# Two 128-byte pads in SBUF and a new order of the router's dot products in the last dense pass

## Chip, core and metric

The kernel runs on one core of a Trainium2 chip. The metric is device time in microseconds for one execution. Before the change the median of three runs is 737.13 us (736.93 to 737.21).

## What is computed

The reference chains three parts over 1,536 tokens of width 512. Only the last two bear on the change:

```python
x = attention(q, k, v, lam)                      # decayed linear attention, N=1536 x D=512
p = domain_probs / domain_probs.sum(-1)          # dense mixture, 4 experts
x = sum(p[:, e] * (relu(x @ w1[e]) @ w2[e]) for e in range(4))
logits = x @ w_gate                              # router of the second mixture, 8 experts
expert = argmax(logits); gate = softmax(logits)[expert]
out[token] = gate * (relu(x[token] @ v1[expert]) @ v2[expert])
```

The dense mixture sends every token through four experts with 1,024 hidden columns. The second mixture sends a token to one of eight experts, so the router's choice for every token must be known before its rows can be gathered by expert.

## The kernel before, in words

Tokens are held in 12 tiles of 128: tiles 0 to 5 are the first half, 6 to 11 the second. The accumulator `acc` (L100) holds per tile 512 sums and two more columns, the gate and the token's number. Matmuls are in fp32r, each product split in a high and a low part, so a product takes three matmuls.

The dense mixture runs in passes over half experts. The first pass and the last are plain; the 13 passes between them are "fast units" (`fast_unit`, matmuls on L754) with fewer products, on sums of operands: their moving operands are the halves of `xh`, `xl` and the tiles `t1` to `t4` of 384 columns. The **last pass** handles the second half of the tokens in three pairs of tiles. Each pair runs eight hidden products `h` (`moe1_mm1`, 12 matmuls of 256 columns each, L600), and then two output products (`moe1_mm2`: `y`, 24 matmuls of 512 columns, L600; for the last three tiles `last_dense`: `yz`). Below the tiles of the three pairs are a and b (6 and 7), c and d (8 and 9), y and z (10 and 11).

PSUM is given out from a ring of three banks (`ps_mm`): a product needs the bank of the third product before it, and that bank is free only when VectorE (DVE) has read it last. Behind a hidden product ScalarE (ACT) makes the high part (L607) and VectorE the low part `ht_..l` (L608); behind an output product VectorE adds it to `acc` (L641; L672 for `last_dense`).

After each product a **hook** runs steps that are written out by hand in a table, `plan`. In the last pass hook 0 to 7 stand behind the hidden products of the first pair, 8 and 9 behind its outputs; 10 to 19 are the second pair's; 20 to 27 are the hidden products of the third. Hooks `(KL - 2, 18)` and `(KL - 2, 19)` stand behind the last two outputs of the last fast unit. What a hook issues goes into each engine's queue in that order, and each engine works its queue strictly in order.

The steps of the table:

- `logit_v` (L866), called a **router sum** here: one VectorE instruction that multiplies a tile's 512 columns of `acc` with one expert's router row and adds them up, with a short read of the total behind it. A tile needs eight of them, one for each expert. For tiles a, b and c they follow the tile's last addition to `acc`. For d, y and z they are made on `acc` as it is before the last pass's addition, and the matmuls of `last_dense` supply the rest; they must only come before that addition. Router rows 0 to 2 lie in tiles `row0` to `row2` (loaded by `open_last`, L840), the others in `x2`. The load inside `logit_v` runs for tile 5 alone.
- `route_choose` (L928 to L946): maximum, choice and one-hot of a tile, six short VectorE instructions and one on GpSimd (POOL).
- `route_send` (L950 to L983): two tiny matmuls for the rank (L953, L955), one ScalarE exponential, three short VectorE instructions, four short GpSimd instructions, and a GpSimd scatter of the tile's rows (L123). The routed half starts with a load of what all scatters of tiles 0 to 9 have written.
- `wg_columns`: the router's columns for `last_dense`.

Of the kernel before, what the change touches and what calls it, by code (L numbers as in the profile page):

```python
# [8 lines left out]
F32 = mybir.dt.float32  # L9
# [9 lines left out]
P = 128  # L19
# [23 lines left out]
KL = K1 - 1  # L43
# [33 lines left out]
def body(ctx: ExitStack, tc: tile.TileContext, lam, att, dp, w1a, w2a, wgt, w1b, w2b, out):  # L77
# [3 lines left out]
    def pool(name, bufs, **kw):  # L81
        return tc.tile_pool(name=name, bufs=bufs, **kw)
# [5 lines left out]
    accp = ctx.enter_context(pool("accp", 1))  # L88
# [9 lines left out]
    ones = const.tile([P, P], BF16, name="ones")  # L98
    desc = const.tile([P, E2], F32, name="desc")
    acc = accp.tile([P, NC, W], F32, name="acc")  # L100
    rk_all = const.tile([P, NC], F32, name="rk_all")
    m2_all = const.tile([P, NC], F32, name="m2_all")
    tiles_e = const.tile([P, E2], F32, name="tiles_e")
# [698 lines left out]
    def open_routing():  # L802
        op = ctx.enter_context(pool("order", 1, side="right"))
        for name, n, d in (
            ("places", EN, F32), ("caps", EN, F32), ("count", E2, F32), ("place", EN, F32),
            ("cap_e", E2, F32), ("lw", 2 * FC * E2, F32), ("nth", EN, I32),
            ("tmp", E2 * max(OMAX, E2), F32),
        ):
            od[name] = op.tile([P, n], d, name=name)
        G.iota(  # L810
            od["places"], pattern=[[1, EN]], base=0, channel_multiplier=0,
            allow_small_or_imprecise_dtypes=True,
        )
        G.memset(od["cap_e"][:, 0:1], float(CAPS[0]))
        for i in range(EN):
            G.memset(od["caps"][:, i:i + 1], float(BY_RANK[i]))
        rp = rt["rs"] = ctx.enter_context(pool("rs", 2, side="right"))
        rt["sm"] = [rt_ctx.enter_context(pool("ps_sm", 1, space=PSUM))]
        rt["none"] = rp.tile([P, W - DM], F32, name="none", bufs=1)
        G.memset(rt["none"], 0.0)  # L820
        G.memset(rt["none"].bitcast(I32)[:, 1:], FAR)
# [308 lines left out]
    with tc.manual_schedule():  # L1130
# [104 lines left out]
        def att_rest():  # L1235
            c = done.pop("rest", None)
            if c is not None:
                att_within(c, 1)
                at_t.pop((c, "v"))
                load_kv(c + 3, "v")  # L1240
                done["c"] = c
            if done["c"] == NC - 1 and "end" not in done:
                done["end"] = 1
                at_ctx.close()
                open_routing()
                open_fast()
# [49 lines left out]
        def at(hook, what, *args):  # L1296
            plan.setdefault(hook, []).append(lambda: what(*args))
# [11 lines left out]
        a, b, c = TT, TT + 1, TT + 2  # L1309
        d, y, z = NC - 3, NC - 2, NC - 1  # L1310

        def at_logits(hook, *now):
            for t, es in now:
                for e in es:
                    at(hook, logit_v, t, e)

        at_logits((KL - 2, 18), (d, (3, 4)))
        at_logits((KL - 2, 19), (d, (5, 6, 7)), (y, (3,)))
        for i, now in enumerate((
            [], [(z, (3,))], [], [(y, (4,))], [], [(z, (4,))], [(y, (5,))],  # L1320
            [(y, (6, 7)), (z, (5, 6, 7))], [(a, range(4))],
            [(a, range(4, 8)), (d, (0,)), (y, (0,))], [(b, (0,))], [(b, (1,))], [(b, (2,))],
            [(b, (3,))], [(b, (4,)), (d, (1,))], [(b, (5,)), (d, (2,))], [(b, (6,)), (z, (0,))],
            [(b, (7,))], [(y, (1, 2)), (z, (1, 2)), (c, (0,))], [(c, (1, 2, 3))], [(c, (4,))],
            [(c, (5,))], [(c, (6,))], [(c, (7,))],
        )):
            if i == 11:
                at(i, route_choose, a)
            at_logits(i, *now)
        at(12, wg_columns)  # L1330
        at(13, route_send, a)
        at(18, route_choose, b)
        at(20, route_send, b)
        at(22, route_send, d)
        at(24, route_choose, c)
# [382 lines left out]
        for e in range(E2):  # L1718
            k = K1 + 2 * e
            load_rows(e + 2)  # L1720
            y = gp.tile([P, NMOST, DM], F32, tag="y", name=f"y{e}")
# [57 lines left out]
    with tc.If(n_r > 0):  # L1779
        with pool("op", 1) as op:  # L1780
# [56 lines left out]
            with tc.For_i(0, n_r, 1) as i:  # L1837
# [34 lines left out]
                y = op.tile([P, DM], F32, name="o_yg")  # L1872
# [69 lines left out]
```

## Time and profile before

| | us |
|---|---|
| median of three runs | 737.13 |
| the profiled execution | 736.41 |
| its span, first to last instruction | 734.60 |
| around the span | 1.81 |
| TensorE matmul busy in the span | 722.9 |
| VectorE busy in the span | 555.7 |

The span is what the trace shows; the profiled execution's own time is 1.81 us longer. TensorE's busy time is the union of its matmuls, whose ends are modelled, so a matmul is read best from its start to the start of the next. Times in the trace are microseconds from the start of the span. The granted clock was 0.997 of full speed on average.

### The profile page before, as it was taken

What the parts mean: (1) busy time and instruction counts of PE and PEld (TensorE: products, weight loads), DVE (VectorE), ACT (ScalarE), POOL (GpSimd) and SP (SyncE); (2) the same over time, 40 slices, a digit from 0 to 9 for tenths busy, and PEclk for the clock granted to TensorE, in tenths of its full rate; (3) what the DMA queues carried; (4) which work ended last, traced back from release to release, by engine and by line L of the source; (5) the groups of instructions that cost most, each with busy time, mean ns of one, the idle gap of its engine ahead of it and who ended that gap; (6) DMA issues with size and microseconds to landing.
All of it is one profiled execution on the core that took longest, in us unless ns stands there. A gap on an engine that the chain in (4) does not pass through costs nothing. (4 is left out here: it accounts for less than half of the span.)

```text
span 734.6 us, 13252 instructions
## 1 busy us (share of the span) xinstructions
PE 722.9 (98%) x4954; PEld 658.1 (90%) x4954; DVE 555.7 (76%) x1287; ACT 310.9 (42%) x689; POOL 95.7 (13%) x137
## 2 busy tenths in 40 slices
PE   9999999999999999999999999999999999999995
PEld 8888989889898988989899897978899998998995
DVE  8557886787879786676878876787898867675884
ACT  4333725343343535424133141531134657565772
POOL 3474000000000000000000003300132013121013
PEclk9999999999999999999999999999999999999998
DMA  8863797728477486555335533362015967865660
GB/s 314 299 220 93 274 267 306 271 94 302 132 270 254 168 321 280 163 238 174 128 130 203 226 127 160 115 192 82 15 52 157 328 219 250 277 202 180 242 235 32
DMA packets 43310, 146.76 MB, mean 200 GB/s; under 512 B 7217, under 2 KB 7217, under 8 KB 38379
## 3 DMA queue, kind: packets, MB, share of 16 engines
q1 hardware_dynamic: 41131, 139.57, 54.7%
q0 software_dynamic: 2112, 6.31, 2.2%
q8 instruction: 40, 0.66, 0.3%
q14 instruction: 27, 0.22, 0.1%
HBM read 111.23 MB, written 34.83 MB: 199 GB/s over the span
## 5 line engine op out<-in xcount | busy, mean ns | idle before, releaser
L211 DVE TENSOR_TENSOR w1l<-raw,w1h 128x512 fp32r<-128x512 f32 x124 | 82.2, 686 | 21.1 <-ACT w1h L209 20.1
L761 ACT COPY u<-b 128x384 f32<-128x384 f32 x78 | 36.8, 477 | 101.0 <-PE b L754 99.9
L641 DVE SCALAR_TENSOR_TENSOR acc<-y,p_sb,acc 128x512 f32<-128x512 f32 x75 | 56.2, 749 | 27.2 <-PE y L600 22.9
L209 ACT CAST w1h<-raw 128x512 fp32r<-128x512 f32 x124 | 72.9, 616 | 1.6 <-DMA raw<-in_w2a 1.6
L936 POOL TENSOR_SCALAR ec<-m_all 128x1 f32<-128x1 f32 x10 | 2.4, 238 | 427.0 <-DVE m_all L933 426.7
L754 PE MATMUL b<-xh,w0h 128*128 128x384 f32 x208 | 57.9, 339 | 0.0
L866 DVE CUSTOM_DVE_ANT_0 x<-acc,x 128x512 f32<-128x512 f32 x78 | 53.6, 687 | 1.3
L211 DVE TENSOR_TENSOR w0l<-raw,w0h 128x512 fp32r<-128x512 f32 x76 | 50.1, 707 | 0.7 <-ACT w0h L209 0.5
L123 POOL DMA_INDIRECT out<-y,xb x16 | 29.3, 1833 | 134.8 <-DVE y L1701 83.7
L768 DVE TENSOR_TENSOR u<-b,u 128x384 f32<-128x384 f32 x78 | 43.0, 551 | 3.8 <-PE b L754 3.8
L209 ACT CAST w0h<-raw 128x512 fp32r<-128x512 f32 x76 | 42.8, 623 | 3.5 <-DMA raw<-in_w1a 3.3
L600 PE MATMUL h<-xh,w0h 128*128 128x256 f32 x144 | 36.1, 292 | 2.7 <-DVE ht_0l L608 2.4
L754 PEld LDWEIGHTS b<-xh,w0h 128*128 128x128 f32 x208 | 38.2, 188 | 0.5
L600 PE MATMUL g<-xg,w0h 128*128 128x288 f32 (+1 forms) x192 | 38.1, 293 | 0.0
L754 PE MATMUL b<-xl,w0h 128*128 128x384 f32 x104 | 35.2, 338 | 0.0
L600 PE MATMUL h<-xh,w0l 128*128 128x256 f32 x144 | 34.7, 283 | 0.1
L754 PE MATMUL b<-t1h,w0h 128*128 128x384 f32 x104 | 31.1, 339 | 0.0
L600 PEld LDWEIGHTS g<-xg,w0h 128*128 128x128 f32 x192 | 30.8, 189 | 0.0
L600 PEld LDWEIGHTS h<-xh,w0h 128*128 128x128 f32 x144 | 26.3, 189 | 4.3 <-DVE ht_0l L608 2.8
L754 PE MATMUL b<-t4h,w0l 128*128 128x384 f32 x104 | 29.1, 340 | 0.0
L754 PE MATMUL b<-t2h,w0l 128*128 128x384 f32 x104 | 29.0, 340 | 0.0
L754 PE MATMUL b<-xh,w0l 128*128 128x384 f32 x104 | 29.0, 339 | 0.0
(370 smaller groups left out, 2139.2 us busy)
## 6 DMA issues: line engine op xcount, KB each, us to landing
raw<-in_w2a SPq DMA_DIRECT2D x32, 512.0 KB, 4.6
raw<-in_w1b SPq DMA_DIRECT2D x32, 512.0 KB, 6.2
raw<-in_w2b SPq DMA_DIRECT2D x32, 512.0 KB, 5.2
kept<-w0h SPq DMA_DIRECT2D x12, 1024.0 KB, 4.2
w0h<-kept SPq DMA_DIRECT2D x12, 1024.0 KB, 7.7
raw<-in_w1a SPq DMA_DIRECT2D x18, 512.0 KB
att<-in_att SPq DMA_DIRECT2D x12, 512.0 KB, 5.0
kept<-w0l SPq DMA_DIRECT2D x6, 1024.0 KB, 7.3
```

Of the source, the lines that this page charges most:

```text
L123: i = G.indirect_dma_start(out=dst, out_offset=bass.IndirectOffsetOnAxis(ap=idx, axis=0), in_=src, in_offset=None, bounds_check=rows - 1, ...
L209: A.copy(out=hi, in_=t)
L211: V.tensor_tensor(out=lo, in0=t, in1=hi.bitcast(F32), op=ALU.subtract)
L600: T.matmul(ps, l, r, start=first and i == 0, stop=last and i == len(ops) - 1)
L641: V.scalar_tensor_tensor(out=acc[:, t, 0:DM], in0=ps, scalar=p_sb[:, t, e:e + 1], in1=acc[:, t, 0:DM], op0=ALU.mult, op1=ALU.add,)
L754: T.matmul(ps, l[:, d, c], r[:, d, :], start=first and i == 0, stop=i == len(ops) - 1, skip_group_check=not first,)
L761: A.copy(out=t, in_=bank[2, s])
L768: V.tensor_tensor(out=t, in0=bank[b, s], in1=t, op=ALU.add)
L866: V.tensor_tensor_reduce(out=x2.rearrange("p d t -> p (d t)")[:, RING * DM:], in0=acc[:, t, 0:DM], in1=rt.get(("row", e), logit_piece(e)), ...
L936: G.tensor_scalar(out=ec, in0=m2, scalar1=-float(MOST), scalar2=float(E2 * MOST), op0=ALU.mult, op1=ALU.add,)
```

## The change

The change makes two tiles that nothing uses, each 32 fp32 columns (128 bytes a partition). `pad_x` lies behind `acc`, in front of everything that the left side of SBUF gets after it (`ht`, `xh`, `xl`, `x2`, and later the routed half's tiles). `pad_t` is made in the pool `rs` at the right side of SBUF, ahead of the pools that follow there (`t1` to `t4`, the units' sums, later the tiles of the routed half). And it rewrites the table of the last pass: the same router sums in another order, `route_choose` of a at hook 17 instead of 11, and `route_send` of a at hook 18 instead of 13.

```diff
     acc = accp.tile([P, NC, W], F32, name="acc")
+    accp.tile([P, 32], F32, name="pad_x")
...
         rt["sm"] = [rt_ctx.enter_context(pool("ps_sm", 1, space=PSUM))]
+        rp.tile([P, 32], F32, name="pad_t", bufs=1)
...
         at_logits((KL - 2, 18), (d, (3, 4)))
-        at_logits((KL - 2, 19), (d, (5, 6, 7)), (y, (3,)))
+        at_logits((KL - 2, 19), (d, (5, 6)))
         for i, now in enumerate((
-            [], [(z, (3,))], [], [(y, (4,))], [], [(z, (4,))], [(y, (5,))],
-            [(y, (6, 7)), (z, (5, 6, 7))], [(a, range(4))],
-            [(a, range(4, 8)), (d, (0,)), (y, (0,))], [(b, (0,))], [(b, (1,))], [(b, (2,))],
-            [(b, (3,))], [(b, (4,)), (d, (1,))], [(b, (5,)), (d, (2,))], [(b, (6,)), (z, (0,))],
-            [(b, (7,))], [(y, (1, 2)), (z, (1, 2)), (c, (0,))], [(c, (1, 2, 3))], [(c, (4,))],
-            [(c, (5,))], [(c, (6,))], [(c, (7,))],
+            [], [(y, (3,))], [], [(d, (7,))], [(z, (3,))], [(y, (4,))], [(z, (4,))],
+            [(d, (0,)), (y, (5, 6, 7)), (z, (5, 6, 7))], [(a, range(8))], [(d, (1,))],
+            [(b, (0,))], [(b, (1,))], [(b, (2,))], [(b, (3,))], [(b, (4,))], [(b, (5,))],
+            [(b, (6,))], [(b, (7,)), (d, (2,)), (y, (0, 1)), (z, (0, 1))],
+            [(y, (2,)), (z, (2,)), (c, (0, 1))], [(c, (2, 3))], [(c, (4,))], [(c, (5,))],
+            [(c, (6,))], [(c, (7,))],
         )):
-            if i == 11:
+            if i == 17:
                 at(i, route_choose, a)
+            if i == 18:
+                at(i, route_choose, b)
             at_logits(i, *now)
         at(12, wg_columns)
-        at(13, route_send, a)
-        at(18, route_choose, b)
+        at(18, route_send, a)
         at(20, route_send, b)
```

In numbers of router sums: hook `(KL - 2, 19)` has 2 instead of 4, hook 7 has 7 instead of 5, hook 8 has 8 instead of 4, hook 9 has 1 instead of 6, hooks 14, 15 and 16 have 1 instead of 2, hook 17 has 6 instead of 1, hook 18 has 4 instead of 5, hook 19 has 2 instead of 3, and hook 4 has 1 instead of none.

## Rows read from the trace of the kernel before

**Rows 1.** The page's part 1: busy us, share of the span, instructions.

```profile
PE 722.9 (98%) x4954; PEld 658.1 (90%) x4954; DVE 555.7 (76%) x1287; ACT 310.9 (42%) x689; POOL 95.7 (13%) x137
```

**Rows 2.** Windows: busy PE, PEld, DVE, ACT, POOL; PEclk; DMA share, GB/s.

```profile
477.50:514.20 36.70, 35.42 (x204) 30.80 (x203) 29.31 (x68) 8.58 (x19) 0.00 (x0) 1.00 0.42 137
514.20:550.90 36.70, 35.47 (x274) 33.86 (x273) 33.16 (x124) 9.62 (x32) 9.56 (x21) 1.00 0.10 33
...
624.40:661.10 36.70, 36.70 (x288) 36.59 (x288) 25.75 (x48) 21.86 (x47) 7.45 (x4) 1.00 0.71 240
```

**Rows 3.** Waits of TensorE from 455 to 560 us: total, times, longest.

```profile
PE h L600 <- DVE ht_0l L608: 2.4, 2, 1.3
```

**Rows 4.** Timeline of TensorE at its first wait: start, us, what, idle before.

```profile
492.74 0.64 PE L600 MATMUL h<-xl,w0h 128*128 128x256 f32 x4
494.66 0.39 PE L600 MATMUL h<-xh,w0h 128*128 128x256 f32 x1 [1.28 <-DVE ht_0l L608]
```

**Rows 5.** Timeline of VectorE ahead of that wait's end.

```profile
491.38 0.68 DVE L866 CUSTOM_DVE_ANT_0 x<-acc,x 128x512 f32<-128x512 f32 x1
...
494.19 0.42 DVE L608 SCALAR_TENSOR_TENSOR ht_0l<-h,ht_0h 128x256 fp32r<-128x256 f32 x1
```

**Rows 6.** Timeline of TensorE at its second wait and at tile a's rank.

```profile
516.95 0.64 PE L600 MATMUL h<-xl,w0h 128*128 128x256 f32 x4
518.73 0.39 PE L600 MATMUL h<-xh,w0h 128*128 128x256 f32 x1 [1.14 <-DVE ht_0l L608]
518.96 0.28 PE L600 MATMUL h<-xh,w0l 128*128 128x256 f32 x1
...
519.79 0.64 PE L600 MATMUL h<-xl,w0h 128*128 128x256 f32 x4
520.47 0.17 PE L953 MATMUL rank<-oh,upper 128*128 128x8 bf16 x1
```

**Rows 7.** Timeline of VectorE ahead of the second wait's end, and tile a's choice.

```profile
513.32 0.75 DVE L641 SCALAR_TENSOR_TENSOR acc<-y,p_sb,acc 128x512 f32<-128x512 f32 x1 [1.91 <-PE y L600]
513.98 0.68 DVE L866 CUSTOM_DVE_ANT_0 x<-acc,x 128x512 f32<-128x512 f32 x1
...
518.26 0.42 DVE L608 SCALAR_TENSOR_TENSOR ht_0l<-h,ht_0h 128x256 fp32r<-128x256 f32 x1
...
519.54 0.15 DVE L928 TENSOR_REDUCE mx<-lg_v 128x1 f32<-128x8 f32 x1
...
520.53 0.68 DVE L866 CUSTOM_DVE_ANT_0 x<-acc,row 128x512 f32<-128x512 f32 x1
```

**Rows 8.** Timeline of TensorE: starts of tile b's output and of the next pair.

```profile
507.53 0.40 PE L600 MATMUL y<-w1h,ht_0h 128*128 128x512 f32 x1
...
513.12 0.28 PE L600 MATMUL h<-xh,w0h 128*128 128x256 f32 x1
```

**Rows 9.** Timeline of VectorE around tile a's last addition.

```profile
502.57 0.42 DVE L608 SCALAR_TENSOR_TENSOR ht_3l<-h,ht_3h 128x256 fp32r<-128x256 f32 x1 [0.41 <-ACT ht_3h L607]
...
507.72 0.75 DVE L641 SCALAR_TENSOR_TENSOR acc<-y,p_sb,acc 128x512 f32<-128x512 f32 x1 [1.18 <-PE y L600]
508.51 0.69 DVE L866 CUSTOM_DVE_ANT_0 x<-acc,row 128x512 f32<-128x512 f32 x1
```

**Rows 10.** Router rows 0 to 2: issue (ns; first and last us); a like transfer's landing.

```profile
L840 SPq DMA_DIRECT2D row<-in_wgt x3: 424/425/432, 491.9 to 492.8; - x3
...
x<-in_wgt SPq DMA_DIRECT2D x13, 256.0 KB, 4.6
```

**Rows 11.** Timeline of POOL: tile a's first step of its send, and its scatter.

```profile
523.49 0.24 POOL L973 TENSOR_SCALAR far<-rk_all 128x1 f32<-128x1 f32 x1 [3.02 <-DVE gs L980]
...
525.65 1.59 POOL L123 DMA_INDIRECT bins<-acc,pos  x1 [0.28 <-POOL pos L979]
```

**Rows 12.** The page's part 5: fastest and slowest group of the units' matmuls.

```profile
L754 PE MATMUL b<-xl,w0h 128*128 128x384 f32 x104 | 35.2, 338 | 0.0
...
L754 PE MATMUL b<-t4h,w0l 128*128 128x384 f32 x104 | 29.1, 340 | 0.0
```

## The prediction

> **What bounds the kernel now.** I read the page's busy line first: TensorE is busy 98% of the span and VectorE 76% [rows 1]. So only what makes TensorE wait can move the time by much. The table of windows shows where it is not full: two stretches of 36.7 us, from 477.5 to 550.9, with 35.42 and 35.47 us busy; a later stretch is full, though its DMA share is 0.71 [rows 2]. The granted clock is 1.00 in all three. The waits of TensorE name one cause for that place, twice: a hidden product waits for a low part on VectorE, 2.4 us in all [rows 3].
>
> The timelines give the true price, from start to start. In a dense run a 256-column matmul starts every 0.12 us. The group of four at 492.74 should have been followed at 493.22; the next started at 494.66, so 1.44 us are lost [rows 4]. The second wait: due at 516.95 + 0.48 = 517.43, started at 518.73, 1.30 us lost. The matmul behind a wait takes 0.23 us to its follower instead of 0.12, so add 0.11 for each. A third, small loss: tile a's rank is due at 519.79 + 0.48 = 520.27 and starts at 520.47, 0.20 us late [rows 6].
>
> Why VectorE was late: its queue is in order, and the low part stood behind router sums. At the first wait four sums run from 491.38 to the low part at 494.19, 2.81 us [rows 5]; at the second six take 513.98 to 518.26, 4.28 us [rows 7]. Hence a sum costs (4.28 - 2.81) / 2 = 0.735 us. The low part is due for a reason: the fourth hidden product needs the bank that the first one's low part sets free. The rank waited because tile a's choice, at 519.54 [rows 7], stood behind all this too.
>
> **The change, part by part.**
>
> *The first wait.* Two of four sums leave the hook ahead of it. The low part starts 2 x 0.735 = 1.47 us earlier, at 492.72, and takes 0.42 us: free at 493.14, due at 493.22. The wait goes, with 0.08 us to spare: gain 1.44 + 0.11 = **1.55 us**. What is late next: nothing by more than a few hundredths, and a wait this short would cost those and 0.11.
>
> *The sums that went.* Up to hook 7 the pair has 7 sums more than hook 7's low part needs: the new table puts one each into hooks 1 and 3 to 6. The hidden products come every 12 x 0.12 = 1.44 us, and VectorE needs 0.735 and a low part of about 0.34 (start to next start), so it keeps up; in hooks 0 to 3 a weight split (0.60) stands there as well, as before. I walked the queue: the tightest low part there is free 0.4 us before it is due.
>
> *Hooks 7 and 8.* The pair's last low part starts at 502.57 in the old trace [rows 9], 1.54 us earlier in the new. Behind it now stand seven sums: 501.03 + 0.34 + 7 x 0.735 - 0.11 (the last one needs no gap) = 506.4. Tile a's output ends at 507.53 - 1.55 = 505.98 [rows 8], and its addition was at 507.72, 0.19 behind the stream; so the addition would start at 506.4, some 0.2 late. Nobody waits for that: its bank is wanted only by the second hidden product of the next pair, at 513.0. Then eight sums, the first 0.79 behind the addition [rows 9]: 506.4 + 0.79 + 8 x 0.735 - 0.11 = 512.9. Tile b's addition is due at 511.8, so it runs 1.1 us late and frees its bank at 513.65. The third hidden product of the next pair wants that bank at 513.12 - 1.55 + 2 x 1.44 = 514.45 [rows 8]. **0.8 us to spare.** This is the new narrow place.
>
> *The second wait.* At hook 9 one sum stands where six stood. The low part starts at about 512.9 + 0.66 + 0.62 = 514.2, is free at 514.6, and due at 517.43 - 1.55 = 515.88: gone, 1.3 us to spare. Gain 1.30 + 0.11 = **1.41 us**.
>
> *Tile a's choice and send.* The choice (0.99 us, from 519.54 to the next sum at 520.53 [rows 7]) goes to hook 17 and the rank to hook 18, some four microseconds behind the choice. The rank's two matmuls cost TensorE the same there; their late start, **0.20 us**, goes. POOL needs 523.49 to 527.24, 3.75 us, for a's steps and scatter [rows 11]. They now come at about 534 and end by 538, ahead of b's send (hook 20, at about 539); the two short choice steps of b and d on POOL keep clear of the scatter or stand behind it without being wanted. The load of all scattered rows waits for c's scatter, at hook 26, whose place is not changed. SP gets no new work: the load inside `logit_v` runs for tile 5 alone.
>
> *Hooks 17 to 19.* Behind the pair's last low part come the choice and six sums, 5.4 us, against 5.59 us for tile c's output [rows 8]: c's addition is up to 0.6 us late, its bank not wanted for 5 us more. Hook 18 has b's choice, four sums and a's send, 4.3 us; d's two additions then run about as late as before, and their banks are free 1.5 us before they are wanted. Hook 19 has two sums, not three.
>
> *Router rows.* Their first use moves from tile a's sums at 508.51 [rows 9] to hook 7, at 501.4. The last was issued at 492.8, and transfers of that size landed after 4.6 us [rows 10]: 497.4. Covered by 4 us; without the cover hook 7 would be that much later.
>
> *The pads.* They remove and add no instruction; they move operands by 128 bytes. No run shows the same tile in another place. The nearest rows are the units' matmuls: twelve groups on `xh`, `xl` and `t1` to `t4`, all between 338 and 340 ns [rows 12]. I take 0. The bounds: 1 ns to either side of 339 over 13 x 14 x 6 = 1,092 of them, 1.1 us of gain or loss.
>
> *The sum.* 1.55 + 1.41 + 0.20 = 3.16 us off the profiled execution's 736.41, so 733.25. The three runs' median lies 0.72 above that execution, so I forecast 737.13 - 3.16 = **733.97 us**, 0.43% faster. The gain should last, since TensorE is full behind this place [rows 2] and the loads there follow buffers that its own work frees. As a test I walked the old table with the same prices: it gives waits of 1.44, 1.36 and 0.21 us at the same three places, and none elsewhere; the new table gives none.
>
> **The rivals.**
>
> *The waits come back at the narrow places.* If VectorE is 1 us later than my walk, the first low part keeps TensorE waiting 0.92 + 0.11, and tile b's bank 0.2 + 0.11: 1.3 us of the gain go, **735.3 us**. For it: margins of 0.08 and 0.8 us. Against: the walk meets the old waits within 0.1.
>
> *The gain is lost further on.* If something on its own clock, the scattered rows' load or a weight load, ends the next wait, TensorE stands there instead: **737.1 us**, the same. For it: the load of scattered rows hangs on a chain through VectorE, POOL and DMA. Against: the full TensorE of the later stretch, and that this chain starts at hooks that move along with TensorE.
>
> *The pads make TensorE's reads slower* (the case of the other side). The place is every matmul that streams `xh`, `xl` or `t1` to `t4`: the 1,092 and 36 x 12 = 432 hidden ones, 1,524. It decides from 3.16 / 1,524 = 2.1 ns each, as much as the groups' whole spread [rows 12]. At 4 ns it costs 6.1 us: **740.1 us**. Against: these operands already lie in many places, with 2 ns between them. The other way, 1 ns less on each gives 1.5 us: **732.4 us**. [...]
>
> *The pads move nothing*, since nothing uses them: then the forecast is unchanged, as I count them as 0.
>
> **How the numbers follow.** Forecast (733.2 to 734.8): 0.70. Waits come back, 735.3: 0.08. Pads help, 732.4: 0.04. Gain lost, 737.1: 0.10. Pads hurt, 740.1: 0.08. The range takes in the pads' bound below, 733.97 - 1.1 = 732.8, a little more for the spread of runs, 732.7, and the first rival above, 735.4; what it leaves out holds 0.2. A measurement can tell about 0.2%, 1.5 us, from no change. The first three cases are faster by more: 0.82. Same: 0.10. Slower: 0.08.
>
> **What would show it.** Right: TensorE's waits for `ht_0l` are absent between 490 and 550; the low part behind hook `(KL - 2, 19)` follows two sums; tile b's addition starts about 1.1 us behind its output's end, and the third hidden product of the next pair still starts on time; the groups on L754 stay between 338 and 340 ns. Wrong: a wait for L641 or L608 at another hook, a wait for the scattered rows near 557, or start-to-start times of the units' matmuls that moved by 2 ns or more.

## The result and the profile after

The changed kernel takes **729.58 us** in the median (729.5 to 730.33, six runs) against 737.03 us (736.32 to 737.28) for the kernel before beside it: a ratio of 0.9903, with a 95% interval of 0.9891 to 0.9916. It is 7.45 us faster, where 3.16 were forecast, and the time lies below the predicted range. The profiled execution took 729.56 us.

The page's head and part 1 of the changed kernel (busy us, share, instructions), for [rows 1]:

```profile
span 727.8 us, 13249 instructions
PE 718.5 (99%) x4954; PEld 654.0 (90%) x4954; DVE 556.4 (76%) x1287; ACT 311.3 (43%) x689; POOL 95.2 (13%) x137
```

The number of matmuls is the same and their busy time fell by 4.4 us. The span less the busy time fell from 11.7 to 9.3 us, by the 2.4 us of the two waits [rows 3]; the fall in busy time comes on top of them, so something else happened. The windows, for [rows 2]:

```profile
477.50:514.20 36.70, 36.70 (x229) 32.87 (x229) 33.59 (x84) 8.78 (x21) 0.00 (x0) 1.00 0.38 123
514.20:550.90 36.70, 36.70 (x291) 35.30 (x290) 33.61 (x127) 11.83 (x33) 11.86 (x25) 1.00 0.20 60
624.40:661.10 36.70, 36.70 (x282) 35.95 (x281) 20.46 (x40) 17.05 (x38) 4.18 (x3) 1.00 0.67 220
```

Both stretches that were not full are full now. The waits of TensorE over the whole run (total us, times, longest), for [rows 3]:

```profile
PE warm L1130 <- POOL ones L1143: 1.0, 1, 1.0
PE g L1557 <- DVE xg L1497: 0.2, 1, 0.2
PE xo L535 <- DVE a L468: 0.2, 1, 0.2
```

Nothing waits for `ht_0l` any more. TensorE's timeline at the places of [rows 4, 6 and 8]:

```profile
489.71 0.64 PE L601 MATMUL h<-xl,w0h 128*128 128x256 f32 x4
490.24 0.39 PE L601 MATMUL h<-xh,w0h 128*128 128x256 f32 x1
490.46 0.28 PE L601 MATMUL h<-xh,w0l 128*128 128x256 f32 x1
...
508.55 0.28 PE L601 MATMUL h<-xh,w0h 128*128 128x256 f32 x1
...
511.39 0.28 PE L601 MATMUL h<-xh,w0h 128*128 128x256 f32 x1
...
512.34 0.63 PE L601 MATMUL h<-xl,w0h 128*128 128x256 f32 x4
512.81 0.28 PE L601 MATMUL h<-xh,w0h 128*128 128x256 f32 x1
```

At the first wait's place the next group starts 0.53 us behind the group of four, not 1.92, and its follower 0.22 behind it: 0.06 late and a slow start, the small remainder that the forecast had allowed for. At the second (512.34 to 512.81) there is none. VectorE's timeline at the same places, for [rows 5, 7 and 9]:

```profile
489.77 0.42 DVE L609 SCALAR_TENSOR_TENSOR ht_0l<-h,ht_0h 128x256 fp32r<-128x256 f32 x1
...
503.40 0.75 DVE L642 SCALAR_TENSOR_TENSOR acc<-y,p_sb,acc 128x512 f32<-128x512 f32 x1
504.19 0.69 DVE L868 CUSTOM_DVE_ANT_0 x<-acc,row 128x512 f32<-128x512 f32 x1
...
509.94 0.75 DVE L642 SCALAR_TENSOR_TENSOR acc<-y,p_sb,acc 128x512 f32<-128x512 f32 x1
510.61 0.68 DVE L868 CUSTOM_DVE_ANT_0 x<-acc,row 128x512 f32<-128x512 f32 x1
511.21 0.42 DVE L609 SCALAR_TENSOR_TENSOR ht_0l<-h,ht_0h 128x256 fp32r<-128x256 f32 x1
```

Tile b's output ends where the next pair starts, 508.55, and its addition comes 1.39 us later, 1.20 more than the usual 0.19. Its bank is free at about 510.7, and the third hidden product that wants it starts on time at 511.39.

The other part shows in the units, which lie long before the last pass. The page's part 5, the same two groups as [rows 12]:

```profile
L755 PE MATMUL b<-xl,w0h 128*128 128x384 f32 x104 | 35.0, 337 | 0.0
...
L755 PE MATMUL b<-t4h,w0l 128*128 128x384 f32 x104 | 28.8, 338 | 0.0
```

TensorE's timeline at one unit of 84 matmuls, its first matmul and the first behind it:

```profile
140.18 0.34 PE L755 MATMUL b<-xh,w0h 128*128 128x384 f32 x1
...
154.75 0.39 PE L601 MATMUL y<-w1h,ht_000h 128*128 128x512 f32 x1
```

And the same two matmuls in the kernel before:

```profile
140.43 0.34 PE L754 MATMUL b<-xh,w0h 128*128 128x384 f32 x1
...
155.27 0.39 PE L600 MATMUL y<-w1h,ht_000h 128*128 128x512 f32 x1
```

The mean durations of the twelve groups moved by 1.7 to 2.5 ns, and matmuls overlap (337 ns of duration, 173.5 from one start to the next), so they are a weak witness. From start to start the unit took 14.84 us before and takes 14.57 after: 176.7 ns a matmul, then 173.5, in a unit where TensorE waits for nothing and the edit changed no instruction.

### The profile page after: what moved, and what is told of

Same layout as the page of the kernel before. It is cut to its first block, busy times and chain, and to the rows that moved or that the text cites. A ratio compares the mean times of both kernels' runs of the same rounds, so it can differ in the third digit from the quotient of the medians.

```text
span 727.8 us, 13249 instructions
## 1 busy us (share of the span) xinstructions
PE 718.5 (99%) x4954; PEld 654.0 (90%) x4954; DVE 556.4 (76%) x1287; ACT 311.3 (43%) x689; POOL 95.2 (13%) x137
## 5 line engine op out<-in xcount | busy, mean ns | idle before, releaser
L755 PE MATMUL b<-t3h,w0h 128*128 128x384 f32 x104 | 28.6, 336 | 0.0
```

Source lines behind the costliest of these rows:

```text
L755: T.matmul(ps, l[:, d, c], r[:, d, :], start=first and i == 0, stop=i == len(ops) - 1, skip_group_check=not first,)
```

## The experiments

The question after the result: did the new order give more than forecast, did the pads give the rest, or was the whole run shorter for some other reason? And once the pads were seen to act: which property of the place? All kernels here compute the same output. Letters in the expectations stand for theories, as each text puts them. The time of the kernel before is always from runs made beside those of the kernel in question.

### Order alone, pads alone

`e1_order_only` is the changed kernel without the two pads; `e2_pads_only` is the kernel before with them.

```diff
-    accp.tile([P, 32], F32, name="pad_x")
-        rp.tile([P, 32], F32, name="pad_t", bufs=1)
```

> The new order of the router sums without the two pads. Theory A (the order takes the waits away; the place of the moving operands in SBUF, moved by the pads from 128 past a multiple of 256 bytes onto one, makes the matmuls that stream them shorter): the two waits and the late rank stay away, so 737.0 - 3.2 = 733.8 us, and the units' 384-column matmuls start every 176.6 ns as before, the hidden 256-column ones on xl every 119.9. Rival B (the faster matmuls belong to the order or to the run, the pads do nothing): 729.6 us and 173.4 ns.

> The two pads without the new order. Theory A: the waits of TensorE for the low part stay (2.4 us by the view of waits, 3.2 from start to start), the units' matmuls start every 173.4 ns and the hidden ones on xl every 118.1, so 1,092 x 3.2 ns + 0.65 us = 4.1 us off, 732.9 us. Rival B: 737.0 us and 176.6 ns.

Measured: order alone 732.89 us against 736.56, ratio 0.9952 (0.9935 to 0.9968), 3.67 us faster. Pads alone 732.98 us, ratio 0.995 (0.9934 to 0.9967), 3.58 us faster. Together 7.25: the two parts add up to the whole of 7.45. Waits of TensorE in the order alone, whole run:

```profile
PE warm L1128 <- POOL ones L1141: 1.0, 1, 1.0
PE h L600 <- ACT xh L180: 0.3, 1, 0.3
PE qk L397 <- DMA att<-in_att: 0.3, 1, 0.3
```

and in the pads alone:

```profile
PE h L601 <- DVE ht_0l L609: 2.6, 2, 1.4
...
PE rank L955 <- DVE oh L936: 0.2, 1, 0.2
```

The order takes the two waits away, the pads leave them. The same matmul's start in the three traces less its start in the kernel before shows where each part's gain is made (us; worked out from the start times of the same matmul in each trace, counted from the span's start):

```
at (before)  order alone   pads alone   both
   253          -0.0            -        -1.3
   465          -0.0          -2.65      -2.8
   495          -1.5          -2.8       -4.4
   520          -2.9          -2.9       -6.0
   541          -3.0          -3.0       -6.4
   578          -3.6          -2.7       -6.7
   end          -3.6          -2.9       -6.9
```

(The profiled execution of the pads alone was the longest of its runs, 733.54 us, so its column ends below the 3.58 of the medians; it also has a wait of 0.5 us for a load, `px` behind `xe` near 558, that the other traces lack.) The pads' gain grows steadily through the units; the order's comes in two steps of 1.47 and 1.37 us at the two waits, then 0.17 by 541 and 0.5 in small late starts by 578 (the rank of tile d at 548.3 and `px` at 560.4, some 0.2 each, and a `g` at 565.2, 0.1).

### One pad at a time

`e3_pad_x` keeps only the pad behind the accumulator, `e4_pad_t` only the one in front of the units' sums.

> The new order and pad_x alone. Theory A: only matmuls that stream xh and xl get shorter, 520 of the units' (173.4 ns) and the hidden ones, while those on t1 to t4 stay at 176.6: 733.8 - 520 x 3.2 ns - 0.65 = 731.5 us. Rival B: as e1 within 0.3 us, with no difference between the groups.

> The new order and pad_t alone. Theory A: only the 572 matmuls on t1 to t4 get shorter (173.4 ns), those on xh and xl stay at 176.6 and the hidden ones on xl at 119.9: 733.8 - 572 x 3.2 ns = 732.0 us. Rival B: as e1 within 0.3 us, no difference between the groups.

Measured: 731.84 us, 0.9939 (0.9923 to 0.9956), and 731.57 us, 0.9933 (0.9916 to 0.9949); that is 1.05 and 1.32 us below the order alone. Mean start-to-start times of the units' matmuls settle it: with `pad_x` those on `xh` and `xl` take 174.2 ns and those on `t1` to `t4` stay at 176.6; with `pad_t` it is 176.3 and 173.6. Each pad shortens the matmuls whose moving operand it moves, and no others. In the times the two single gains make 2.37 us, where both pads together took off 3.3 (729.58 against 732.89): the runs with `pad_x` alone lie 1.1 us apart, and with `pad_t` alone the output matmuls took 0.4 us longer in all, so the times of single pads are a rougher measure here than the matmuls.

### Other widths

The two widths in columns of four bytes, `pad_x` and `pad_t`: 16 and 64 in `e5_x64_t256`, 8 and 16 in `e6_x32_t64`, 24 and 24 in `e7_x96_t96`, 40 and 48 in `e8_x160_t192`, 24 and 40 in `e10_x96_t160`, 24 and 32 in `e12_x96_t128`. The pattern of the edit:

```diff
-    accp.tile([P, 32], F32, name="pad_x")
+    accp.tile([P, 24], F32, name="pad_x")
-        rp.tile([P, 32], F32, name="pad_t", bufs=1)
+        rp.tile([P, 24], F32, name="pad_t", bufs=1)
```

> As the changed kernel, but pad_x of 64 bytes (xh and xl start 192 bytes behind a multiple of 256) and pad_t of 256 (t1 to t4 start 128 behind one, as before the change, 256 bytes further down). Theory A (the start's place within 256 bytes counts): the units' matmuls on t at 176.6 ns, as before; those on xh and xl longer than 173.7. Rival C (any pad helps, since it sets these tiles apart from their neighbours): both near 173.5.

> pad_x of 32 bytes (start at 160 within 256) and pad_t of 64 (start at 64). Theory A: neither group reaches 173.5; where the cost of other starts lies is read here, and by the y matmuls (starts at 64 and 192 take 2 to 3 ns more than the others) the t group would be the longest so far, 177 or more. Rival C: both near 173.5.

> pad_x and pad_t of 96 bytes (starts at 224 and at 32 within 256). Theory A: both longer than 173.5, up to 176.6. Rival C: both near 173.5.

> pad_x of 160 bytes (start at 32 within 256) and pad_t of 192 (start at 192). Theory A: x as the t group of the run with pads of 96 (the same place, 32), t as the x group of the run with a pad of 64 (192): the place decides and not the tile. Rival C: both near 173.5.

> pad_x of 96 and pad_t of 160 bytes: all moving operands of the units start at 224 within 256. Theory A1 with one rule for all tiles: the t groups take 174.3 ns, as xh and xl at 224 did. If they take 176.5 instead, as t1 to t4 at 192 did where xh and xl took 174.4, the place within 256 bytes alone does not decide, and something that differs between the tiles does too.

> The best place of each seen so far: xh and xl at 224 (pad_x 96 bytes), t1 to t4 at 0 (pad_t 128). Theory A1: xh and xl 174.3, t 173.4 ns, hidden matmuls 116.2 instead of 118.2; against the run with both pads of 96 only t gains, 572 x 0.5 ns = 0.3 us, so 727.5 us, 2 us under the changed kernel. If the gain of that run was a chance of its one execution: 729.5 us.

Measured: 730.54, 732.24, 727.83 and 730.82 us for the first four (one time each, the kernel before 735.98); 729.72 for `e10_x96_t160` (one time) and 728.14 (727.84 to 728.26) for `e12_x96_t128`, ratio 0.9888 (0.9871 to 0.9904), with the kernel before at 736.36. A pad is no good by being there: `pad_x` of 32 and `pad_t` of 64 bytes (`e6_x32_t64`) leave the units as slow as before, 176.3 and 176.5 ns, while a `pad_x` of 64 (`e5_x64_t256`) gives 174.4. `t1` to `t4` moved by 256 bytes in `e5_x64_t256` stand at 176.6 again, as if they had not been moved; since several places are that slow, this alone does not show a period of 256. Two expectations failed by group: in `e8_x160_t192` `t1` to `t4` at start 192 took 176.5 ns where `xh` and `xl` at 192 had taken 174.4, and in `e10_x96_t160`, with all starts at 224, the groups took 175.7 and 175.4, neither of the two values that were named. So the operand's own start is not the whole rule.

### Which property of the place

The next three kernels move the weights or everything. `e9_weights_96` has `xh`, `xl` and `t1` to `t4` at the places of the changed kernel and moves the weights `w0` 96 bytes on. `f2_all_96` moves the operands and the weights by 96 bytes together (and takes `zero` from `x2` to make room). `f1_w1_96` leaves those places and moves `w1`, the raw weights and `acc`.

```diff
 # e9: pad_x narrower by as much
-    accp.tile([P, 32], F32, name="pad_x")
+    accp.tile([P, 8], F32, name="pad_x")
+    const.tile([P, 24], F32, name="pad_w")
 # f2: pad_w as in e9, pad_x left at 32
+    const.tile([P, 24], F32, name="pad_w")
-        rp.tile([P, 32], F32, name="pad_t", bufs=1)
+        rp.tile([P, 8], F32, name="pad_t", bufs=1)
 # f1: pad_x 8 columns, pad_w behind w0, in front of w1
+        wp.tile([P, 24], F32, name="pad_w", bufs=1)
```

> As the changed kernel, with xh, xl and t1 to t4 at the very same addresses, but all weight tiles 96 bytes further (start 128 within 256 instead of 32). Theory A1 (the moving operand's own start counts): 173.5 ns on both groups, as in the changed kernel. Rival A2 (what counts is the distance of the moving operand from the weights that are loaded beside it): the distance is then as in no fast case so far, and both groups go to 176 or more.

> The units' weights AND their moving operands all 96 bytes further than in the changed kernel: weights at 128, xh, xl and t1 to t4 at 96 within 256, their distance unchanged. (The zeros that start the decay tables lie in x2's first columns, which makes the room.) Theory A2: 173.5 ns on both groups. Theory A1 (own start counts): 176 or more, since 64, 128 and 160 took that.

> Of what the run with the weights 96 bytes further had moved, the units' weights w0 stay in place (32 within 256), and the output weights w1, the raw weights and the accumulator alone move by 96. xh, xl and t1 to t4 are where the changed kernel has them. Theory A2 (the place of the moving operand against the weights loaded beside it): 173.5 ns on both groups, as in the changed kernel. Rival A4 (what other engines and transfers touch beside it, as the raw weights and the accumulator, counts): 176, as in that run.

Measured, one time each: 732.75 us for `e9_weights_96` (before: 736.36), 729.10 for `f2_all_96` and 729.02 for `f1_w1_96` (before: 736.5). The same unit's first matmul and the one behind it, in `e9_weights_96`:

```profile
141.07 0.34 PE L756 MATMUL b<-xh,w0h 128*128 128x384 f32 x1
...
155.86 0.40 PE L602 MATMUL y<-w1h,ht_000h 128*128 128x512 f32 x1
```

and in `f2_all_96`:

```profile
139.84 0.34 PE L756 MATMUL b<-xh,w0h 128*128 128x384 f32 x1
...
154.41 0.39 PE L602 MATMUL y<-w1h,ht_000h 128*128 128x512 f32 x1
```

and in `f1_w1_96`:

```profile
139.93 0.34 PE L755 MATMUL b<-xh,w0h 128*128 128x384 f32 x1
...
154.51 0.40 PE L601 MATMUL y<-w1h,ht_000h 128*128 128x512 f32 x1
```

14.79, 14.57 and 14.58 us. With the operands at the very addresses of the changed kernel the gain is gone once `w0` moves away; with operands and weights moved alike it is all there. `w1`, the raw weights and `acc` have no part in it: they lie at the same places in `e9_weights_96` and `f1_w1_96`, which differ in `w0` alone. So it is not where the operand lies by itself, but where it lies **relative to the weights** `w0`. What makes the distance count is not shown: the mean duration of the units' weight loads is 188 ns in the kernel before and in the changed kernel alike, and `w0` is also written by ScalarE and VectorE, up to 264 us of the changed kernel's trace. Only two runs move `w0`, both by 96 bytes.

`e11_xl_alone` puts `xl` at the good place and leaves `xh` at the old one. `f4_pitch` keeps the changed kernel's places and changes the row pitch of the `w1` tiles.

```diff
 # e11, instead of pad_x, between xh and xl
+    xp.tile([P, 32], F32, name="pad_l")
 # f4: rows of the w1 tiles without their gap, except in the last blocks
+            pitch = HF + E2 * (b[0] and KL - 1 <= b[1] <= KL)
-                wp.tile([P, 4, HF + E2 * b[0]], F32R, ...)
+                wp.tile([P, 4 * (HF + E2 * b[0])], F32R, ...)[:, :4 * pitch].rearrange(
+                            "p (c f) -> p c f", c=4)
```

> No pad behind the accumulator, but one of 128 bytes between xh and xl, and pad_t of 128: xh starts at 128 within 256, xl at 0. Theory A1: matmuls on xl take 173.5 ns, those on xh 176.6. Rival A3 (the step from one matmul's operand to the next one's counts): both groups in between, about 175, since nearly every matmul on one is followed by one on the other.

> As the changed kernel, but the rows of w1 lie 2,048 bytes apart instead of 2,080, except in the last pass: so the 512-column moving operands of y all start at one place within 256 (32 in one buffer, 160 in the other) instead of at eight. Theory A3 (a step between places from one matmul to the next costs): y falls from 232.8 to about 229 ns, where the line through 256 and 384 columns puts it, so 1,080 x 4 ns = 4 us off, 725.5 us. Theory A2: their distance from the stationary ht tiles becomes 32 and 160, both among the slow ones for t, so y stays at 232 to 235 and the time at 729 to 731 us.

Measured: `e11_xl_alone` 730.87 us (one time; before 736.36): the units' matmuls on `xh` and on `xl` both take 176.1 ns. `xl` did not gain from a place that is good when `xh` is there too, so its own place is not enough. Either what stands next to a matmul in the stream counts as well, or something else that `pad_x` moves with `xh`, such as `ht`, does. This is not explained. `f4_pitch` took 730.23 us (730.15 to 730.27), 0.9915 (0.9898 to 0.9931): the output matmuls `y`, 233.9 ns on average in the changed kernel, take 234.5 here, 0.6 us more in all. The idea that a step between places from one matmul to the next decides (theory A3) had asked for about 229, and falls.

The places in one table, without `e11_xl_alone` and without further kernels at places that are listed. Distance is the start of the moving operand less the start of `w0`, modulo 256 bytes (the author's choice; no run shows the period), from the program's allocation of SBUF; ns are mean start-to-start times from the traces (gaps of 220 ns and more, for `h` 150, are waits or slow starts and left out), `h` for the hidden products' matmuls on `xl`, 256 columns:

```
run               x: distance  ns     t: distance  ns      h ns
before                   96  176.6            96  176.7   119.9
e1_order_only            96  176.6            96  176.7   120.2
changed kernel          224  173.7           224  173.4   118.1
f2_all_96               224  173.7           224  173.4   118.5
e3_pad_x                224  174.2            96  176.6   118.2
e4_pad_t                 96  176.3           224  173.6   120.1
e5_x64_t256             160  174.4            96  176.6   118.1
e6_x32_t64              128  176.3            32  176.5   119.3
e7_x96_t96              192  174.3             0  173.9   116.1
e8_x160_t192              0  173.8           160  176.5   119.8
e9_weights_96           128  176.2           128  176.0   119.2
e10_x96_t160            192  175.7           192  175.4   116.0
e12_x96_t128            192  174.4           224  174.0   116.0
```

Where a distance occurs twice for the same operands the times agree within 0.6 ns, with one exception: 192 for `x` gives 174.3 and 174.4, but 175.7 when `t` is at 192 too. The distances that the runs with moved weights have in common with others agree as well: 128 gives 176.3 in `e6_x32_t64` and 176.2 in `e9_weights_96`. At 160 `x` and `t` differ, 174.4 and 176.5; counted modulo 512 these two are 160 and 416, so a longer period than 256 may be behind it, which no run tests.

### The best place

`e7_x96_t96` was the quickest of the widths, so it ran again as `g1_both_96`, with the changed kernel as `g2_after_again` beside it.

> The fastest of the pad sizes so far, both pads of 96 bytes, timed in rounds. By its one execution 727.8 us, 1.7 us under the changed kernel (hidden 256-column matmuls 116.2 ns, not 118.2, on 432 of them 0.9 us; 256-column ones of the routed half 113.9, not 118.3). If that was chance: as the changed kernel beside it.

> The changed kernel itself, for the comparison on the same chip: 729.6 us, units' matmuls 173.7 and 173.4 ns.

Measured: **727.93 us** (727.63 to 728.52), 0.9884 (0.9868 to 0.9901), against 729.18 us (728.98 to 729.5), 0.99 (0.9883 to 0.9916). The ranges do not meet: pads of 96 bytes beat both kernels, the changed one by 1.25 us. The sums of start-to-start times say how: the units' matmuls lose 0.6 us to the changed kernel, the hidden ones gain 0.7, the output ones 0.75 and the routed half's `g` 0.6. The first wait of the last pass is back there by 0.2 us: the next group starts 0.66 us behind the group of four (488.66 to 489.32), where four starts of the 116.1 ns that the hidden products took in `e7_x96_t96`, the same kernel, make 0.46. That VectorE's queue is what they come too quickly for is the author's estimate.

## Why the prediction was wrong

**The first wait, The second wait, Tile a's choice and send: right.** Forecast 1.55, 1.41 and 0.20 us, 3.16 in all; the order alone gave 1.47 and 1.37 at the two waits, 0.17 up to 541, and 3.67 us in the medians. The 0.5 beyond 541 are small waits where the walk of the queue had found none, such as the rank of tile d (the 0.2 us that the pads alone still show). The margin of 0.08 us at the first low part held in the order alone, where the next group starts 0.48 us behind the group of four; in the changed kernel, whose hidden products come quicker (118.1 ns where the order alone has 120.2), it costs 0.06 and the slow start behind it, as was said such a wait would. The rival in which the waits come back at 1 us of error did not happen; the walk of the queue met the traces to about 0.1 us.

**Hooks 7 and 8: right.** Tile b's addition was to be 1.1 us late and 0.8 us ahead of need; it was 1.2 late with 0.7 to spare. **Hooks 17 to 19** and **Router rows**: no wait of TensorE appears for them. POOL had tile a's steps and scatter where the forecast put them (534, less the 3 us that the pads had gained by then), out of the way of tile b's, the last line:

```profile
530.89 0.24 POOL L975 TENSOR_SCALAR far<-rk_all 128x1 f32<-128x1 f32 x1 [3.21 <-DVE gs L982]
...
532.55 1.10 POOL L124 DMA_INDIRECT bins<-acc,pos  x1 [0.58 <-DVE df L942]
...
535.43 0.24 POOL L975 TENSOR_SCALAR far<-rk_all 128x1 f32<-128x1 f32 x1 [1.07 <-DVE gs L982]
```

**The pads: the step that failed.** "I take 0. The bounds: 1 ns to either side of 339 over 13 x 14 x 6 = 1,092 of them, 1.1 us of gain or loss." The measured size, over all gaps, the few long ones included, is 2.7 ns on 468 matmuls, 1.28 us, 3.0 ns on 624, 1.88 us, and 0.57 us in the hidden products: 3.7 us of shorter matmuls, of which 3.6 showed in the pads alone and 3.3 to 3.8 on top of the new order (by the times, and by each one's gain over the kernel before beside it). Two readings led there. First, the duration of a matmul was taken as the measure where the same text had used start to start for the waits; durations overlap and are modelled, and moved by only 1.7 to 2.5 ns. Second, the rival of slower reads was set aside because "these operands already lie in many places, with 2 ns between them". They did not: in the kernel before, all of them have the same distance of 96 to `w0` (modulo 256 bytes), so their agreement had no contrast in it and could not bound anything. The rival of pads that help was priced at 1 ns and a chance of 0.04. The sign that the text had named for a wrong forecast, start-to-start times of the units' matmuls that moved by 2 ns or more, is the one that came.

**The rival of slower reads.** Its chance of 0.08 and its price of 4 ns were estimates of the author. The slowest mean of the units' matmuls in the table, 176.7 ns, is that of the places before; no new place was slower. What does count is the place of the weights: the matmuls on `xh` and `xl` take 173.8 ns in `f1_w1_96` and 176.2 in `e9_weights_96`, with only the place of `w0` to tell the two apart. Which access to `w0` makes the difference, no run here shows.

**What stays open:** the mechanism, the full rule of good and bad distances and its period, why `xl` alone gains nothing, why `x` loses at 192 when `t` is there too, and why `y` never gets shorter by more than 1 ns.

## What to carry to other kernels

Where TensorE is full, compare start-to-start times of one dense group between two kernels before calling a move of tiles free, and ask whether the rows that seem to bound it differ in the thing that is moved. Two small unused tiles that shift moving operands against the weights are a cheap thing to try on a matmul-bound fp32r kernel, in several widths, since the gain is not known beforehand; of the widths tried here none made the units' matmuls slower than before. The hand-written order could be forecast here by walking the in-order queue with start-to-start prices, short by 0.5 us; margins of under 0.1 us should be taken as none.

## What the hardware showed beyond that

A dense fp32r matmul of 384 columns takes from 173.4 to 176.7 ns from start to start, and one of 256 columns in the hidden products from 116.0 to 120.2, by the place of its operand against the weights: 1.9% and 3.5%, with the granted clock at 1.00 in every window of 36.7 us of the kernel before and of the changed one up to 697.9 us, and at 0.996 to 0.998 over the whole of each run. The two sizes do not agree on the best place: a distance of 0 gives 173.8 ns for 384 columns and 119.8, near the worst, for 256. The routed half's first products of 256 columns went from 119.9 ns before to 118.2 in the changed kernel and 114.1 in `g1_both_96`, the largest step seen, 4.8% in all.
